# Where the next batch's projections stand among attention's score tiles

## The chip, the cores and the metric

The kernel runs on one core of one Trainium2 chip. The metric is the time of one execution on the device, in microseconds. Three runs of the kernel before took 1319.05, 1314.22 and 1311.92 us; the median is 1314.22 us.

## The reference, cut to what matters

Three blocks follow each other, all in float32, for 8 batches of 576 tokens.

```python
# 1: linear attention, per head (8 heads of 64, 128 features)
proj = x @ w_phi; proj -= max|proj|; phi = [exp(proj), exp(-proj)]
x1 = (phi(q) @ (phi(k).T @ v)) / (phi(q) @ sum(phi(k)) + 1e-6)
# 2: mixture of 4 attention experts, two of them taken per token
q, k, v = x1 @ wq[e], x1 @ wk[e], x1 @ wv[e]
a = softmax(causal(q @ k.T / 8)); ye = a @ v @ wo[e]
x2 = sum over the two best e of gate[e] * ye          # gate from x1 @ w_gate
# 3: token-shift feed-forward
xk, xr = mu * x2 + (1 - mu) * x2_shifted_by_one_token
out = sigmoid(xr @ w_r) * (relu(xk @ w_k) ** 2 @ w_v)
```

## The kernel before

Every product of block 2 and 3 is made of three passes over operands split into a high and a low part (`mm3`, L113). Four generators, called streams here, emit the work, and `weave` (L54) interleaves them by costs that each step returns:

- `favors` (L640) is block 1, for one batch after the other. Its tiles on TensorE (PE) are `pj` (projection by `w_phi`), `kv`, `tq` (transposes), `num` and `xt`; the last writes the batch's x1, split, into the store `XT`.
- `moe1` (L398) is block 2. Per batch and pair of experts (`ep` is 0 or 1) `qk_tasks` makes four tasks of 12 matmuls each into tiles `qk`, two for the queries, two for the keys; `v_tasks` makes five tasks of 12 matmuls into tiles `vp` (values and gate logits of all four experts), and `gate` turns the logits into weights on VectorE (DVE). Then `s_task` follows for each of 2 experts x 5 score tiles: scores `sc` on PE (L508, L509), mask and maximum on DVE (L518, L522), exponential on ScalarE (ACT, L528), reciprocal on DVE (L534), scaling on GpSimd (POOL, L540), transposes `at` back on PE (L547), and their copies into the tiles `at1h`/`ath` on ACT and `at1l`/`atl` on DVE. `av_task` multiplies the result by the values (`yp`, L582), and at a pair's end writes it to DRAM (`yd<-yt`, L603, on the SyncE queue, SP).
- `gates_keys` (L676) is the first product of block 3 (and `wo`, folded into its weights by `compose`, tiles `fo`). It goes by six chunks of 768 tokens. A chunk has 36 steps of 6 matmuls, tiles `rk`; before them `load_y` (L666) reads the chunk from DRAM into the one buffer `yc_` by four transfers issued on ACT's queue (L673). The buffer's name has a number per chunk: `yc__7491`, `yc__9926`, `yc__12263`, `yc__13856`, `yc__14845` and `yc__15948` are chunks 0 to 5 of the kernel before; the changed kernel has its own numbers. Each `rk` step's weights `wt` come by a transfer on ACT's queue too, its result goes to DRAM by SP (`kd<-z`).
- `moe2` (L727) is the rest: loads `kx<-kd` and `zs<-kd` on SP, relu and square on ACT, the split on DVE, and matmuls `vacc`, 192 a chunk. Its accumulators and most of its buffers take the place of block 2's, so it can't start before the last tile of `moe1` is done.

Within `moe1` the list of tasks sets the order (L611 to L638), and `skewed` (L41) overlaps the stages of neighbours in that list. What `weave` emits is a priority. The framework's own scheduler then sets each engine's order from priorities, dependencies and a model of durations, so moving a task in the list also moves other streams' instructions. `compose`, the weight decoding and `rk` carry a lower priority and fill PE where the others have nothing ready. Score tiles share two PSUM buffers; `qk`, `vp`, `at` and `yp` share two others until `favors` has ended, and after that `qk`, `vp` and `yp` have two of their own (`TAGS`, `LATE`, L31).

In the kernel before, the list has in front of the ten score tiles of a pair all projections of the following pair: four `qk` tasks in front of the first pair's score tiles, and four `qk`, five `vp` and the gate of the next batch in front of the second pair's.

Of the kernel before, what the change touches and what calls it, by code (L numbers as in the profile page):

```python
# [14 lines left out]
B, S, H, D = (8, 576, 8, 64)  # L15
# [61 lines left out]
def fused_kernel(ctx: ExitStack, tc: tile.TileContext, qT, kT, vx, wphi, wq, wk, wvg, wo, mu, w64, ident, cmask, tri, out):  # L77
# [25 lines left out]
    def evac(e, o, i):  # L103
        if e == 'a':
            nc.scalar.activation(o, i, AF.Copy)
        else:
            nc.vector.tensor_copy(o, i)
    state = {}

    def tg(n):  # L110
        return dict(tag=LATE.get(n, TAGS[n]) if 'favored' in state else TAGS[n], bufs=2)

    def mm3(ps, pairs, first=True, last=True):  # L113
        n = 3 * len(pairs)
        i = 0
        for sh, sl, mh, ml in pairs:
            for a, m in ((sh, mh), (sh, ml), (sl, mh)):
                nc.tensor.matmul(ps, a, m, start=first and i == 0, stop=last and i == n - 1)  # L118
                i += 1
# [278 lines left out]
    def moe1():  # L398

        def qk_tasks(b, ep):  # L400

            def one(isk, c):
                cs = slice(288 * c, 288 * c + 288)
                d = {}

                def mm():
                    if not isk and c == 0:
                        QS[b, ep] = pA.tile([P, 2, S], F32R, name='qs', tag='qs', bufs=2)
                        K1[b, ep] = pA.tile([P, 2, S], F32R, name='k1', tag='k1', bufs=2)
                        K2[b, ep] = K2Z[ep]  # L410
                    ps = psA.tile([P, 288], F32, name='qk', **tg('qk'))
                    wh, wl = (wkh, wkl) if isk else (wqh, wql)
                    mm3(ps, [(wh[:, ep, kt], wl[:, ep, kt], xh[kt, b][:, cs], xl[kt, b][:, cs]) for kt in (3, 2, 1, 0)])
                    d['ps'] = ps
                    if isk and c == 1 and (ep == 1):
                        read.add(b)
                    return 12 * 123

                def ev():
                    ps = d['ps']  # L420
                    for j in range(2):
                        r = slice(64 * j, 64 * j + 64)
                        o = slice(64 - 64 * j, P - 64 * j)
                        if isk:
                            k1 = K1[b, ep]
                            nc.scalar.activation(k1[r, j, cs], ps[r], AF.Copy)
                            nc.scalar.activation(k1[o, j, cs], ps[r], AF.Copy)
                            nc.vector.tensor_sub(K2[b, ep][r, j, cs], ps[r], k1[r, j, cs].bitcast(F32))
                        else:
                            q_ = QS[b, ep]  # L430
                            nc.scalar.activation(q_[r, j, cs], ps[r], AF.Copy, scale=0.125)
                            nc.vector.scalar_tensor_tensor(q_[o, j, cs], ps[r], 0.125, q_[r, j, cs].bitcast(F32), op0=OP.mult, op1=OP.subtract)
                return [(lambda: written.get(b, 0) == NHP * S, mm), ev]
            return [one(k, c) for k in range(2) for c in range(2)]

        def v_tasks(b):

            def one(t):
                m = P if t < 4 else 64
                d = {}  # L440

                def mm():
                    if t == 0:
                        VS[b] = VSP[b % 2]
                        LG[b] = pA.tile([P, 5, E], F32, name='lg', tag='lg', bufs=2)
                        nc.vector.memset(LG[b][64:P, 4, :], 0.0)
                    ps = psA.tile([P, 260], F32, name='vp', **tg('vp'))
                    cs = slice(P * t, P * t + m)
                    mm3(ps[:m], [(xh[kt, b][:, cs], xl[kt, b][:, cs], wvh[:, kt], wvl[:, kt]) for kt in (3, 2, 1, 0)])
                    d['ps'] = ps  # L450
                    return 12 * 109

                def ev():
                    ps = d['ps']
                    v4 = ps[:m, :256].rearrange('p (e d) -> p e d', e=E)
                    evac('a', VS[b][:m, t, :, 0:64], v4)
                    nc.vector.tensor_sub(VS[b][:m, t, :, 64:128], v4, VS[b][:m, t, :, 0:64].bitcast(F32))
                    nc.vector.tensor_copy(LG[b][:m, t, :], ps[:m, 256:260])
                return [mm, ev]
            return [one(t) for t in range(5)]  # L460

        def gate(b):

            def go():
                l = LG[b]
                sh4 = [P, 5, E, E]
                lf = l.unsqueeze(2).to_broadcast(sh4)
                le = l.unsqueeze(3).to_broadcast(sh4)
                g1 = pA.tile([P, 5, E, E], F32, name='g1', tag='g1')
                g2 = pA.tile([P, 5, E, E], F32, name='g2', tag='g2')  # L470
                nc.vector.tensor_tensor(g1, lf, le, op=OP.is_gt)
                nc.vector.tensor_tensor(g2, lf, le, op=OP.is_equal)
                nc.vector.tensor_mul(g2, g2, trs.rearrange('p (e f) -> p e f', e=E).unsqueeze(1).to_broadcast(sh4))
                nc.vector.tensor_add(g1, g1, g2)
                rk = pA.tile([P, 5, E], F32, name='rk', tag='rk')
                nc.vector.tensor_reduce(rk, g1, axis=AX.X, op=OP.add)
                mx = pA.tile([P, 5], F32, name='mx', tag='mx')
                nc.vector.tensor_reduce(mx, l, axis=AX.X, op=OP.max)
                sh3 = [P, 5, E]
                w_ = pA.tile([P, 5, E], F32, name='gw', tag='gw', bufs=2)  # L480
                nc.vector.tensor_sub(w_, l, mx.unsqueeze(2).to_broadcast(sh3))
                nc.scalar.activation(w_, w_, AF.Exp)
                nc.vector.scalar_tensor_tensor(w_, rk, 1.5, w_, op0=OP.is_lt, op1=OP.mult)
                sm = pA.tile([P, 5], F32, name='gs', tag='gs')
                nc.vector.tensor_reduce(sm, w_, axis=AX.X, op=OP.add)
                nc.vector.tensor_scalar_add(sm, sm, 1e-09)
                nc.vector.reciprocal(sm, sm)
                nc.vector.tensor_mul(w_, w_, sm.unsqueeze(2).to_broadcast(sh3))
                WT[b] = w_
            return [None, None, go]  # L490
# [116 lines left out]
        plan = []  # L607
# [3 lines left out]
        tasks = []  # L611
        due = []

        def flush(force=False):
            due.sort(key=lambda x: x[0])
            while due and (force or due[0][0] <= len(tasks)):
                tasks.append(due.pop(0)[1])
        tasks += qk_tasks(0, 0) + v_tasks(0) + [gate(0)]
        for n, (b, ep) in enumerate(plan):
            if n + 1 < len(plan):  # L620
                nb, nep = plan[n + 1]
                tasks += qk_tasks(nb, nep)
                if nep == 0:
                    tasks += v_tasks(nb) + [gate(nb)]
            for e in (2 * ep, 2 * ep + 1):
                for i in range(5):
                    tasks.append(s_task(b, e, i))
                    flush()
                    if i == 1:
                        due.append((len(tasks) + 5, av_task(b, e, 0)))  # L630
                    if i == 4:
                        due.append((len(tasks) + 4, av_task(b, e, 1)))
        while due:
            if due[0][0] > len(tasks):
                tasks.append([lambda: 2400])
            flush()
# [90 lines left out]
    def moe2():  # L727
# [62 lines left out]
        return skewed(tasks)  # L790
    clear_pads()
    fs, ms, rk, m2 = (favors(), skewed(moe1()), skewed(gates_keys()), moe2())
    for _ in range(3):
        next(fs)
# [57 lines left out]
```

## Time and profile before

| | |
|---|---|
| median of three runs | 1314.22 us |
| profiled execution | 1317.01 us, its span 1315.2 us |
| PE busy | 1257.2 us (96%) |
| VectorE / ScalarE / GpSimd busy | 881.4 / 732.5 / 411.6 us |
| matmuls | 9152 |

The span is the stretch from the first instruction to the last. Busy is the union of an engine's instructions; matmuls overlap, and so a stretch in which PE is busy throughout may still be paced by something else. `favors` starts its last `xt` at 822.1 us, the last `yp` of block 2 ends at 1051 us, and from then on only `rk` and `vacc` run on PE.

### The profile page before, as it was taken

Reading aid. Unit: us, or ns where it says so; the run is one execution under the profiler, and the core shown is the slowest. Engines: PE = TensorE matmul, PEld = TensorE weight load, DVE = VectorE, ACT = ScalarE, POOL = GpSimd, SP = SyncE. Lnnn points to the kernel's source line nnn. Section 1 sums busy time; section 2 is a strip of 40 time slices with the busy share of each in tenths; the row PEclk is TensorE's granted clock in tenths of the full one; section 3 lists DMA queues with packets and bytes.
Section 4 is the critical chain, followed back from the end, with each engine's and each line's share of the span. In section 5 each row is a group of like instructions: output and inputs, shape, how many; then the busy total and the mean of one; then the engine's idle time right before and its main releaser. Section 6 shows DMA issues by size and latency. Waiting matters only on the chain.

```text
span 1315.2 us, 26615 instructions
## 1 busy us (share of the span) xinstructions
PE 1257.2 (96%) x9152; PEld 1207.0 (92%) x9152; DVE 881.4 (67%) x2477; ACT 732.5 (56%) x1836; POOL 411.6 (31%) x570
## 2 busy tenths in 40 slices
PE   7999999999999999999999999898997989999998
PEld 7999899899999999899989999887996989999998
DVE  7776885887886777787777678565676745443442
ACT  5665675677676556565556556654454556343330
POOL 5541562655453335333433323322112200000000
PEclk9999999899999999999999999998997999999999
DMA  6322141324053435434554456578466897778741
GB/s 183 88 86 81 59 131 51 109 68 136 27 176 118 140 95 173 140 111 124 170 181 117 136 149 211 172 217 259 146 214 213 262 314 244 255 258 283 241 143 66
DMA packets 174358, 208.77 MB, mean 159 GB/s; under 512 B 19728, under 2 KB 159376, under 8 KB 174224
## 3 DMA queue, kind: packets, MB, share of 16 engines
q1 hardware_dynamic: 96656, 136.28, 31.7%
q10 hardware_dynamic: 77568, 70.79, 18.5%
q8 instruction: 74, 1.21, 0.4%
q14 instruction: 60, 0.49, 0.1%
HBM read 143.58 MB, written 63.44 MB: 157 GB/s over the span
## 4 chain that ended last, share of the span: by engine, by line
PE 76%; DVE 7%; DMA 5%; ACT 4%; POOL 3%; issue 2%; ACTq 1%; POOLq 0%; SPq 0%; DVEq 0%
PE vacc L118 14%; PE rk L118 14%; PE kv L328 9%; PE num L366 8%; PE qk L118 7%; PE vp L118 4%; PE at L547 3%; PE yp L582 3%; PE pj L276 3%; PE fo L118 2%; DMA kd<-z 2%; PE pj L278 2%; PE pj L277 2%; PE sc L508 2%; PE tq L350 2%
## 5 line engine op out<-in xcount | busy, mean ns | idle before, releaser
L118 PE MATMUL vacc<-XT,wvh 128*128 128x384 f32 x768 | 197.1, 338 | 2.1 <-DVE o L779 2.1
L101 POOL TENSOR_TENSOR lo<-raw,hi 128x256 fp32r<-128x256 f32 (+1 forms) x160 | 109.9, 691 | 259.9 <-ACT hi L98 217.5
L540 POOL TENSOR_SCALAR a<-a,rc,gw 128x128 f32<-128x128 f32 (+4 forms) x160 | 107.0, 671 | 202.6 <-DVE rc L534 109.8
L366 PE MATMUL num<-kvs,ph 128*128 128x65 f32 (+1 forms) x1280 | 142.8, 264 | 4.6 <-DVE xs L373 4.4
L366 PEld LDWEIGHTS num<-kvs,ph 128*128 128x128 f32 (+1 forms) x1280 | 137.5, 182 | 10.3 <-DVE xs L373 6.2
L118 PEld LDWEIGHTS vacc<-XT,wvh 128*128 128x128 f32 x768 | 139.8, 189 | 2.4 <-DVE o L779 2.4
L706 DVE TENSOR_TENSOR z<-rk,z 128x384 f32<-128x384 f32 x144 | 79.5, 552 | 74.3 <-PE rk L118 34.4
L286 DVE TENSOR_REDUCE m<-pj 128x4 f32<-128x512 f32 (+1 forms) x160 | 100.6, 631 | 41.9 <-PE pj L278 40.1
L118 PE MATMUL vacc<-XT,wvl 128*128 128x384 f32 x384 | 128.2, 338 | 0.0
L528 ACT ACTIVATE a<-sc,nm 128x128 f32<-128x128 f32 (+2 forms) x192 | 98.1, 514 | 45.4 <-DVE nm L522 16.1
L288 DVE TENSOR_TENSOR pm<-pj,m 128x512 f32<-128x512 f32 (+1 forms) x160 | 99.5, 627 | 1.4
L276 PE MATMUL pj<-wph,hi 128*128 128x256 f32 x288 | 92.4, 321 | 6.9 <-DVE wpl L101 3.8
L522 DVE TENSOR_REDUCE nm<-sc 128x1 f32<-128x128 f32 (+2 forms) x192 | 87.4, 468 | 3.9 <-PE sc L509 2.1
L98 ACT ACTIVATE hi<-raw 128x256 fp32r<-128x256 f32 (+1 forms) x160 | 61.8, 392 | 41.9 <-PE pj L277 19.3
L278 PE MATMUL pj<-wph,lo 128*128 128x256 f32 x288 | 84.0, 292 | 0.7 <-POOL lo L101 0.7
L277 PE MATMUL pj<-wpl,hi 128*128 128x256 f32 x288 | 83.5, 290 | 0.0
L547 PE MATMUL at<-idn,a 128*128 128x128 f32 (+2 forms) x480 | 74.5, 265 | 5.5 <-POOL a L540 2.9
L508 PE MATMUL sc<-k,qs 128*128 128x128 f32 (+2 forms) x192 | 66.2, 351 | 12.7 <-ACT a L528 12.6
L754 ACT ACTIVATE kx<-kx 128x768 f32<-128x768 f32 x48 | 40.2, 842 | 62.1 <-DMA kx<-kd 50.7
L563 ACT ACTIVATE at1h<-at 128x384 fp32r<-128x384 f32 (+3 forms) x128 | 53.5, 419 | 38.0 <-PE at L547 17.1
L118 PEld LDWEIGHTS vacc<-XT,wvl 128*128 128x128 f32 x384 | 72.5, 189 | 0.0
L100 DVE CAST XT<-kx 128x768 fp32r<-128x768 f32 x48 | 26.7, 557 | 65.4 <-PE vacc L118 53.6
(464 smaller groups left out, 3441.4 us busy)
## 6 DMA issues: line engine op xcount, KB each, us to landing
wt<-wf ACTq DMA_DIRECT2D x216, 256.0 KB, 3.7
kd<-z SPq DMA_DIRECT2D x144, 192.0 KB, 3.4
kx<-kd SPq DMA_DIRECT2D x48, 384.0 KB, 4.4
yd<-yt SPq DMA_DIRECT2D x16, 864.0 KB, 4.7
zs<-kd SPq DMA_DIRECT2D x24, 384.0 KB, 5.6
out_dram<-o SPq DMA_DIRECT2D x24, 384.0 KB, 4.6
raw<-in_kT_dram SPq DMA_DIRECT2D x64, 128.0 KB, 2.1
raw<-in_qT_dram SPq DMA_DIRECT2D x64, 128.0 KB, 2.2
```

The source lines that it names most:

```text
L101: (el or nc.vector).tensor_sub(lo, src, hi.bitcast(F32))
L118: nc.tensor.matmul(ps, a, m, start=first and i == 0, stop=last and i == n - 1)
L276: nc.tensor.matmul(o, hi[:, c], wph, start=True, stop=False)
L277: nc.tensor.matmul(o, hi[:, c], wpl, start=False, stop=False)
L278: nc.tensor.matmul(o, lo[:, c], wph, start=False, stop=True)
L286: nc.vector.tensor_reduce(m[:, :g], ps, axis=AX.X, op=OP.max, apply_absolute_value=True)
L288: nc.vector.tensor_sub(pm[:, :g * P].rearrange('p (g f) -> p g f', f=P), ps, m[:, :g].unsqueeze(2).to_broadcast([P, g, P]))
L328: nc.tensor.matmul(bank[:, r, :], d['kp'][:, r % 2, c0:c0 + P], d['v'][:, i + (lo_ > 0), r // 2, :], start=new and r == 0, stop=end, skip_ ...
L366: nc.tensor.matmul(ps[lo_:hi_, i, j, :], d['qp'][:, hf, c0 + lo_:c0 + hi_], kvs[hp, b][:, r * 65:(r + 1) * 65], start=hf == 0, stop=hf == 1)
L528: nc.scalar.activation(a[:m, k0:k1_], o, AF.Exp, bias=nm[:m, 0:1], scale=1.0, accum_out=sm[:m, n:n + 1])
L540: eng(asc).tensor_scalar(a[:m, :nk], a[:m, :nk], rc[:m], WT[b][:m, i, e:e + 1], op0=OP.mult, op1=OP.mult)
L547: nc.tensor.transpose(ps[:kw, jj * m:jj * m + m], d['a'][:m, jj * P:jj * P + kw], idn[:m, :m])
```

## The change

The list of `moe1`'s tasks is written in another order. The four `qk` tasks of a batch's second pair are put one by one behind the first four score tiles of the first pair. The next batch's `qk` tasks of its first pair, its five `vp` tasks and the gate are put behind the last score tile of the second pair, with the `av` tasks that fall due among them. No instruction on data is added or taken away.

```diff
--- before.py
+++ after.py
@@ -616,20 +616,22 @@
             while due and (force or due[0][0] <= len(tasks)):
                 tasks.append(due.pop(0)[1])
         tasks += qk_tasks(0, 0) + v_tasks(0) + [gate(0)]
-        for n, (b, ep) in enumerate(plan):
-            if n + 1 < len(plan):
-                nb, nep = plan[n + 1]
-                tasks += qk_tasks(nb, nep)
-                if nep == 0:
-                    tasks += v_tasks(nb) + [gate(nb)]
+        for b, ep in plan:
+            ahead = qk_tasks(b, 1) if ep == 0 else []
             for e in (2 * ep, 2 * ep + 1):
                 for i in range(5):
                     tasks.append(s_task(b, e, i))
                     flush()
+                    if ahead:
+                        tasks.append(ahead.pop(0))
                     if i == 1:
                         due.append((len(tasks) + 5, av_task(b, e, 0)))
                     if i == 4:
                         due.append((len(tasks) + 4, av_task(b, e, 1)))
+            if ep == 1 and b + 1 < B:
+                for t in qk_tasks(b + 1, 0) + v_tasks(b + 1) + [gate(b + 1)]:
+                    tasks.append(t)
+                    flush()
         while due:
             if due[0][0] > len(tasks):
                 tasks.append([lambda: 2400])
```

The first place is ACT at the load of chunk 4 (`yc__14845` before, `yc__14723` in the changed kernel; `a,sm<-sc,nm` is a score tile's exponential). Before:

```order
L673 DMA yc__14845<-yd_112 128x6x192
L563 ACTIVATE at1h<-at 128x3x128
L673 DMA yc__14845<-yd_112 128x6x192
L528 ACTIVATE a,sm<-sc,nm 64x512
L528 ACTIVATE a,sm<-sc,nm 64x64
L563 ACTIVATE at1h<-at 128x4x128
L721 DMA wt<-wf_116 128x2x256
L673 DMA yc__14845<-yd_113 128x6x192 x2
L528 ACTIVATE a,sm<-sc,nm 128x128
L528 ACTIVATE a,sm<-sc,nm 128x256
L563 ACTIVATE at1h<-at 128x4x64
L105 ACTIVATE yc<-yp 64x256
```

Now:

```order
L563 ACTIVATE at1h<-at 64x64
L723 DMA wt<-wf_116 128x2x256
L675 DMA yc__14723<-yd_112 128x6x192 x2
L105 ACTIVATE yc<-yp 64x320
L675 DMA yc__14723<-yd_113 128x6x192 x2
L98 ACTIVATE yt<-yf_172 128x288
L723 DMA wt<-wf_116 128x2x256
L98 ACTIVATE yt<-dl 128x576
L105 ACTIVATE z<-rk 128x384
L723 DMA wt<-wf_116 128x2x256
L723 DMA wt<-wf_117 128x2x256 x2
```

The load stood among the exponentials of score tiles; now it stands behind the last score tile of all, around the copy `yc<-yp` of the last product.

The second place is PE between chunks 2 and 3 (`yc__12263` and `yc__13856` before, `yc__12344` and `yc__13852` now). Before:

```order
L118 MATMUL rk<-yc__12263,wt 128x384 x6
L547 MATMUL at<-idn,a 128x64 x4
L547 MATMUL at<-idn,a 64x64
L118 MATMUL rk<-yc__12263,wt 128x384 x12
L508 MATMUL sc<-k_12013,qs 128x384
L509 MATMUL sc<-k2z_165,qs 128x384
...
L547 MATMUL at<-idn,a 128x128 x2
L508 MATMUL sc<-k_12013,qs 64x512
L509 MATMUL sc<-k2z_165,qs 64x512
L547 MATMUL at<-idn,a 128x128 x3
...
L118 MATMUL rk<-yc__13856,wt 128x384 x2
```

Now:

```order
L118 MATMUL rk<-yc__12344,wt 128x384 x6
L118 MATMUL vp<-wvh,XT 128x260
L118 MATMUL vp<-wvl,XT 128x260
...
L118 MATMUL vp<-wvl,XT 64x260
L118 MATMUL vp<-wvh,XT 64x260 x2
L118 MATMUL vp<-wvl,XT 64x260
L118 MATMUL vp<-wvh,XT 64x260
L118 MATMUL qk<-XT,wqh 128x288 x2
L118 MATMUL qk<-XT,wql 128x288
...
L547 MATMUL at<-idn,a 128x128 x2
L118 MATMUL rk<-yc__13852,wt 128x384 x2
```

Before, 36 matmuls `qk` and 12 `sc`, 10 `yp`, 10 `at` stand between the two chunks; now 48 `qk`, 24 `vp` and 3 `at`, and no score tile.

The third place is PE between chunks 3 and 4 (`yc__13856` and `yc__14845` before, `yc__13852` and `yc__14723` now). Before:

```order
L118 MATMUL rk<-yc__13856,wt 128x384 x12
L547 MATMUL at<-idn,a 128x128 x3
L508 MATMUL sc<-k_13825,qs 64x64
L509 MATMUL sc<-k2z_165,qs 64x64
L582 MATMUL yp<-ath,vsp_168 128x256
L582 MATMUL yp<-ath,vsp_168 128x128
...
L508 MATMUL sc<-k_13825,qs 64x512
L509 MATMUL sc<-k2z_165,qs 64x512
...
L509 MATMUL sc<-k2z_165,qs 64x64
L118 MATMUL rk<-yc__14845,wt 128x384 x2
L547 MATMUL at<-idn,a 128x128 x4
```

Now:

```order
L118 MATMUL rk<-yc__13852,wt 128x384 x12
L582 MATMUL yp<-at1h,vsp_168 128x320 x3
L582 MATMUL yp<-at1h,vsp_168 128x192
L118 MATMUL rk<-yc__13852,wt 128x384 x6
L582 MATMUL yp<-at1h,vsp_168 128x64
L582 MATMUL yp<-at1l,vsp_168 64x320 x3
L582 MATMUL yp<-at1l,vsp_168 64x192
L582 MATMUL yp<-at1l,vsp_168 64x64
L118 MATMUL vacc<-XT,wvh_13239 128x384 x2
...
L118 MATMUL vacc<-XT,wvh_13239 128x384 x2
L118 MATMUL vacc<-XT,wvl_13240 128x384
L118 MATMUL rk<-yc__14723,wt 128x384 x36
L118 MATMUL vacc<-XT,wvh_13239 128x384 x5
```

Before, 14 `sc`, 18 `at` and 18 `yp` stand between the chunks. Now 6 `yp` and 48 `vacc` do, and block 2 ends before chunk 4 begins: 432 matmuls `rk` stand behind the last `yp`, 300 before.

## Rows read from the trace of the kernel before

**Rows 1.** The page's first lines: span, and busy time of TensorE.

```profile
span 1315.2 us, 26615 instructions
...
PE 1257.2 (96%) x9152; PEld 1207.0 (92%) x9152; DVE 881.4 (67%) x2477; ACT 732.5 (56%) x1836; POOL 411.6 (31%) x570
```

**Rows 2.** Stretches: length, PE busy (matmuls), granted clock, DMA share, GB/s.

```profile
60.00:428.00 368.00, 355.78 (x2970) 0.98 0.30 94
428.00:840.00 412.00, 404.78 (x3191) 1.00 0.49 147
840.00:906.00 66.00, 59.67 (x377) 1.00 0.71 224
906.00:924.60 18.60, 12.87 (x72) 0.82 0.60 185
924.60:995.40 70.80, 68.41 (x446) 1.00 0.65 197
995.40:1012.00 16.60, 10.85 (x55) 0.69 0.76 265
1012.00:1053.00 41.00, 40.12 (x243) 0.96 0.74 227
1053.00:1090.00 37.00, 33.64 (x184) 0.95 0.93 319
1137.50:1155.80 18.30, 18.30 (x108) 1.00 1.06 362
```

**Rows 3.** Waits of PE, 840 to 1053 us: total, times, longest.

```profile
PE sc L508 <- ACT a L528: 10.0, 7, 3.2
PE rk L118 <- DVE z L706: 2.8, 4, 1.1
```

**Rows 4.** PE in order of time (start, us, what), inside 906 to 916 us.

```profile
910.30 0.41 PE L547 MATMUL at<-idn,a 128*128 128x128 f32 x2
913.95 0.69 PE L508 MATMUL sc<-k,qs 128*64 128x512 f32 x1 [3.23 <-ACT a L528]
```

**Rows 5.** ACT in order of time, the same stretch; ACTq is its queue.

```profile
907.60 1.73 ACTq L673 DMA_DIRECT2D yc__13856<-yd  x2
...
909.40 3.73 ACTq L673 DMA_DIRECT2D yc__13856<-yd  x1
913.23 0.58 ACT L528 ACTIVATE a<-sc,nm 128x384 f32<-128x384 f32 x1 [3.58 <-issue]
```

**Rows 6.** PE's last and first `rk` around four changes of chunk.

```profile
649.79 0.68 PE L118 MATMUL rk<-yc__7491,wt 128*128 128x384 f32 x3
660.22 0.42 PE L118 MATMUL rk<-yc__9926,wt 128*128 128x384 f32 x1
...
904.03 2.38 PE L118 MATMUL rk<-yc__12263,wt 128*128 128x384 f32 x12
924.53 0.51 PE L118 MATMUL rk<-yc__13856,wt 128*128 128x384 f32 x2
...
993.43 2.33 PE L118 MATMUL rk<-yc__13856,wt 128*128 128x384 f32 x12
1010.91 0.59 PE L118 MATMUL rk<-yc__14845,wt 128*128 128x384 f32 x2
...
1135.79 2.10 PE L118 MATMUL rk<-yc__14845,wt 128*128 128x384 f32 x11
1153.68 0.51 PE L118 MATMUL rk<-yc__15948,wt 128*128 128x384 f32 x2
```

**Rows 7.** The chain that ended last: start, us, what; three unbroken runs of matmuls.

```profile
877.13 1.58 PE qk L118 x12
...
933.03 2.87 PE vp L118 x24
...
1119.12 16.66 PE vacc L118 x96
```

**Rows 8.** DMA issues: count, KB each, median us to landing.

```profile
yc__14845<-yd ACTq DMA_DIRECT2D x4, 576.0 KB, 7.7
```

## The prediction

> **What bounds the kernel now.** I read the page's busy times first: PE is busy for 1257.2 of 1315.2 us [rows 1], no other engine for more than 67%. All matmuls stay, so the change can only move what PE loses. The table of stretches says where that is. Loss in a stretch is here its length less PE's busy time, plus its length times what the granted clock lacks to 1.00. The second part is a bound, since a slow clock costs nothing while PE idles anyway. By that, 60 to 428 us loses 12.2 + 7.4 us, 428 to 840 us 7.2, 840 to 1090 us 36.4 [rows 2]. So a fifth of the span holds more than half of what these rows lose: the part in which only score tiles, projections and `rk` are left for PE.
>
> Inside it, two short stretches stand out. From 906.0 to 924.6 us PE idles 5.7 us at a granted clock of 0.82, a loss of up to 9.1; from 995.4 to 1012.0 us it idles 5.8 us at 0.69, up to 10.9 [rows 2]. (A granted clock of 0.69 means that 62% of the stretch ran at 1.2 and not at 2.4 GHz, behind PE's idle time.) The list of `rk` matmuls tells what these stretches are: in both one chunk ends and the next has to be loaded into the single buffer, 18.1 and 15.2 us from the end of one to the start of the next [rows 6], and during that time PE's filler is gone. The waits name the partner: scores wait 10.0 us, 7 times, for an exponential to free their bank [rows 3]. One such wait lasts 3.23 us [rows 4], and ACT shows why the exponential is late: its queue spends 1.73 us on two and 3.73 us on another of the four load transfers, and the next exponential starts at 913.23 when they are through [rows 5].
>
> **The change part by part.** Nothing is removed or added. What moves are, per batch, 8 `qk` tasks (12 matmuls, two or four ACT copies and two DVE subtractions each), 5 `vp` tasks (12 matmuls, one ACT copy, two DVE operations) and a gate. They issue no transfer. But transfers move against them: the `yd` store on SP of a batch's second pair, which in the list stood behind the next batch's nine tasks, now stands in front of them, so a chunk's data is there earlier. The scheduler also puts other work between chunks now, and by the order of the built programs I go through the changes of chunk.
>
> Prices of cover come from unbroken runs: a `qk` matmul 1.58/12 = 0.132 us, `vp` 2.87/24 = 0.120, `vacc` 16.66/96 = 0.174 [rows 7]. What a chunk's change needs from the end of the last `rk` to the start of the next was 9.8, 18.1, 15.2 and 15.8 us [rows 6]; these are upper bounds, as the first `rk` may have been queued behind other work, and the smallest is the nearest to a bound from below.
>
> 1. Chunk 3 to 4 leaves the score tiles. Between them stood 50 short matmuls of score tiles, with their exponentials behind the load; now it happens when block 2 is over. The 10.9 us fall to what an equal length costs in the stretch behind it, (0.9 + 1.6) us x 16.6/41 = 1.0 [rows 2]. Term: -9.9. Bounds 0 and -10.9.
>
> 2. Chunk 2 to 3 now has 48 `qk` and 24 `vp`, 6.3 + 2.9 = 9.2 us, and no score tile. Against a need of 15.2 us, the row with the nearest DMA load, 6.0 us of waiting are left of 9.1. Term: -3.1. Bounds: need 9.8, only 0.6 left, -8.5; need 18.1, 8.9 left, -0.2. ACT still holds the four transfers, and now copies of `vp` and `qk` queue behind them; PE has two banks of 12 matmuls, 2.9 us, before it feels that.
>
> 3. The change from 3 to 4 moves to the hand-over to `vacc`. There 48 `vacc`, 8.3 us, and 6 `yp`, some 0.6 us, stand between; need 15.2, so 6.3 us are waited. Bounds: 0.9 (need 9.8) and 9.2 (need 18.1). The hand-over's own loss, 3.4 + 1.9 us in 1053 to 1090 us [rows 2], stays. Term: +6.3. Queued behind the first waiting `rk` on PE are 36 `rk` and then all `vacc`; on ACT two of the load's transfers stand before the copy `yc`, two before the split `yt` from which the last store and then the `kx` loads follow.
>
> 4. Chunk 4 to 5 had 92 `vacc` between, 16.0 us, and PE did not idle [rows 2]: the need of 15.8 was just hidden. Now 66 `vacc` stand there, 11.5 us. If that cover is gone, 4.3 us are waited. Term: +4.3. Bounds 0 (need 9.8) and 6.6 (need 18.1).
>
> 5. Chunks 0 to 1 and 1 to 2 have 54 and 54 matmuls between them for 57 and 62, 11 fewer of about 0.13 us. Term: +1.5; bounds 0 and +4 for a need above the cover already, which the first one's 9.8 us suggest.
>
> 6. The rest of 840 to 1053 us loses 6.3 + 2.4 + 2.5 = 11.2 us [rows 2]. Behind the last `xt` the order has 98 score matmuls for 120, so a fifth less of the chains that make these waits. Term: -2.0; bounds +4 (468 matmuls `rk` as filler there for 563) and -6.
>
> 7. Before 840 us 26.8 us are lost [rows 2]. Spread projections put more work between tiles that share two PSUM buffers: pairs of `qk`, `vp`, `at`, `yp` tiles with under 1.5 us of PE work between one use of a buffer and the next fall from 24 to 15 in the order, counted at such prices. No row prices that; a tenth is my choice. Term: -2.0; bounds +8 and -8.
>
> Sum: -9.9 - 3.1 + 6.3 + 4.3 + 1.5 - 2.0 - 2.0 = -4.9 us. The profiled execution took 1317.0 us, 2.8 above the median of the three runs; 1317.0 - 4.9 = 1312.1, and against the median 1314.2 - 4.9 = 1309.3. I forecast **1309 us**. About 0.5%, 6.6 us, is what a measurement of this kernel can tell from no change, so the forecast is a small gain at the edge of that.
>
> **The rivals.** *A larger gain.* The load's need is nearer to 9.8 us, as from chunk 0 to 1, because no exponentials and fewer `wt` transfers share ACT's queue with it. For it speaks that the two long changes are those in which score tiles held PE and so the next `rk`; against it that 15.8 us were needed among `vacc` as well. Terms 2 to 5 become -8.5, +0.9, 0 and +1.5, the sum -20.0, the time 1294; with half of it 1300.
>
> *No change.* The waits are the same ones in other places: terms 2 and 6 at nothing, 3 and 4 at 9.2 and 6.6 from a need of 18.1. Then -9.9 + 9.2 + 6.6 + 1.5 - 2.0 = +5.4, or with term 4 as forecast +3.1: 1317 to 1320.
>
> *Slower: the hand-over.* Chunk 4's load is 4 x 576 KB, 2.36 MB [rows 8]. It now falls where the `kx` and `zs` loads of chunk 0 start, a stretch that moves 319 GB/s at a DMA share of 0.93 already [rows 2]. There 2.36 MB more take 7.4 us, and `kx` lands by that much later while the load itself needs 18.1. PE would wait 9.2 + 7.4 us, and at the clock of the 906 us stretch lose 3.3 more: 19.9 in place of 6.3, a sum of +8.7 and 1323 us. It decides as soon as `kx` lands after the 36 `rk`, some 15 us behind the load's issue. Against it: chunk 5's load at a share of 1.06 cost PE nothing [rows 2]. The Trainium skill ("DMA: Bandwidth & Descriptors", section "Issuing engines are not separate DMA queues") says that transfers started by several engines run on the same 16 DMA engines and interleave, which speaks for this rival. The same section calls the time to initiate a transfer "usually small relative to the DMA itself"; here 3.73 us for one issue stand beside a median landing of 7.7 us, and the measurement decides.
>
> **How the numbers follow.** Forecast, 1303 to 1314 us: 0.46. Larger gain, 1292 to 1303: 0.22. No change, 1314 to 1320: 0.17. Slower: 0.15. Faster by over 0.5% is the larger gain and four tenths of the forecast's case, 0.41; slower by over 0.5% is the hand-over and a little of the third case, 0.17; the rest, 0.42, is within 0.5%. The range of 1297 to 1321 us leaves out the far end of each side; the forecast's own is 1303 to 1314.
>
> **What would show it.** Right: the `sc` waits for an exponential behind 840 us fall from 10.0 to under 4 us; PE idles some 6 us between the 48 `vacc` and the first `rk` of chunk 4, and some 4 us behind the 66 `vacc` before chunk 5; the last `yp` ends some 35 us before its 1051 us, 23 us of that being the 132 `rk` that move behind it. The forecast is wrong if the hand-over loses over 15 us, if chunk 5's first `rk` isn't waited for, or if the loss before 840 us moves by more than 8 us.

## The result and the profile after

The changed kernel takes 1302.86 us (median of 6 runs, 1298.90 to 1306.01) against 1313.42 us: a ratio of 0.9913 over all runs (the two medians alone give 0.9920), 95% interval 0.9885 to 0.9940. Six more runs of it gave 1299.41 us and 0.9893 (0.9868 to 0.9918). So it is faster by about 1%; the forecast was 1309 us, the range 1297 to 1321.

The page of the changed kernel shows as many matmuls as before and a span 18.1 us shorter. Some of that is these two executions: the profiled one was the fastest of its six runs, the one of before 3.6 us above its median.

```profile
span 1297.1 us, 26595 instructions
...
PE 1249.1 (96%) x9152; PEld 1204.4 (93%) x9152; DVE 884.2 (68%) x2477; ACT 733.2 (57%) x1836; POOL 412.5 (32%) x570
```

The table of stretches of the changed kernel (columns as in [rows 2]; 811.2 us is its last `xt`, 1008.5 its last `yp`):

```profile
60.00:428.00 368.00, 359.96 (x3059) 1.00 0.32 100
220.00:260.00 40.00, 38.38 (x325) 1.00 0.26 83
428.00:811.20 383.20, 378.12 (x3020) 1.00 0.45 134
811.20:1008.50 197.30, 178.45 (x1148) 0.98 0.69 212
837.20:850.20 13.00, 9.46 (x55) 0.87 0.77 248
931.80:946.00 14.20, 9.96 (x77) 1.00 0.65 206
1007.00:1020.00 13.00, 11.27 (x59) 0.87 1.00 337
1134.60:1146.20 11.60, 11.60 (x68) 1.00 1.03 334
```

The same view of the kernel before, two stretches that its table in [rows 2] does not have (822.2 us is its last `xt`, 1051 its last `yp`):

```profile
220.00:260.00 40.00, 35.14 (x260) 0.91 0.28 97
822.20:1051.00 228.80, 206.81 (x1295) 0.96 0.68 212
```

Read with the prediction's measure (length less busy, plus length times what the clock lacks), 60 to 428 us lost 12.2 + 7.4 us [rows 2] and now loses 8.0 at a full clock. The stretch with no `favors` left lost 22.0 + 9.2 us and now loses 18.9 + 3.9. So the trace shows two gains, 11.6 and 8.4 us, and the larger is the one that I had all but left out.

Where the early one is, the groups of instructions in 220 to 260 us show (name, count, busy and mean, then idle time before and who ended it). Before:

```profile
L366 PE MATMUL num<-kvs,ph 128*128 128x65 f32 (+1 forms) x95 | 12.0, 287 | 2.5 <-DVE xs L373 2.5
...
L118 PE MATMUL fo<-wth,sw 128*128 128x256 f32 x28 | 6.8, 316 | 1.1 <-ACT wth L98 1.1
```

After:

```profile
L366 PE MATMUL num<-kvs,ph 128*128 128x65 f32 (+1 forms) x96 | 10.8, 262 | 0.0
L118 PE MATMUL vp<-wvh,XT 128*128 128x260 f32 (+1 forms) x40 | 8.1, 292 | 0.4 <-DVE k2z L428 0.4
```

Before, the last of the next batch's `vp` matmuls starts at 218.4 us and the next `qk` at 265.7, so for 46 us PE ran no projection: block 1's chain (`num` waits for `xs`, which DVE makes of the last `num`) had only `fo` and score tiles between its links, PE got through 260 matmuls and its clock fell (0.91 granted). Now 120 matmuls `qk` and `vp` stand there, `num` waits for nothing, and PE gets through 325. By the same measure this stretch loses 8.5 us before and 1.6 now, 6.8 of the 11.6.

The three changes of chunk that the prediction spoke of, by the changed kernel's first and last `rk` (start, length):

```profile
930.68 1.21 PE L118 MATMUL rk<-yc__12344,wt 128*128 128x384 f32 x6
945.99 0.59 PE L118 MATMUL rk<-yc__13852,wt 128*128 128x384 f32 x2
...
1005.88 1.24 PE L118 MATMUL rk<-yc__13852,wt 128*128 128x384 f32 x6
1019.46 1.75 PE L118 MATMUL rk<-yc__14723,wt 128*128 128x384 f32 x9
...
1134.35 0.34 PE L118 MATMUL rk<-yc__14723,wt 128*128 128x384 f32 x1
1146.03 0.62 PE L118 MATMUL rk<-yc__15948,wt 128*128 128x384 f32 x2
```

Beside [rows 6], the gaps from the end of one to the start of the next are 14.1, 12.3 and 11.3 us, for 18.1, 15.2 and 15.8. Behind the 66 `vacc` PE did not idle at all (11.60 of 11.60 us busy).

### The profile page after: what moved, and what is told of

It is laid out like the page before. It is cut to its first block, busy times and chain, and to the rows that moved or that the text cites. A ratio compares the mean times of both kernels' runs of the same rounds, so it can differ in the third digit from the quotient of the medians.

```text
span 1297.1 us, 26595 instructions
## 1 busy us (share of the span) xinstructions
PE 1249.1 (96%) x9152; PEld 1204.4 (93%) x9152; DVE 884.2 (68%) x2477; ACT 733.2 (57%) x1836; POOL 412.5 (32%) x570
## 4 chain that ended last, share of the span: by engine, by line
PE 83%; DVE 6%; DMA 4%; ACT 2%; POOL 2%; issue 1%; ACTq 1%; SPq 0%; DVEq 0%; POOLq 0%
PE rk L118 16%; PE vacc L118 16%; PE kv L328 10%; PE num L366 8%; PE qk L118 6%; PE vp L118 4%; PE yp L582 3%; PE at L547 3%; PE pj L276 3%; PE fo L118 3%; PE pj L278 2%; PE pj L277 2%; PE tq L350 2%; PE sc L508 2%; PE sc L509 2%
## 5 line engine op out<-in xcount | busy, mean ns | idle before, releaser
L118 PE MATMUL vacc<-XT,wvh 128*128 128x384 f32 x768 | 201.2, 338 | 3.8 <-DVE XT L100 2.0
L105 ACT ACTIVATE z<-rk 128x384 f32<-128x384 f32 x72 | 35.2, 489 | 63.0 <-PE rk L118 53.2
```

## The experiments

Two theories stood against each other. *Loads*: the gain comes from the tail, since a chunk's load no longer meets score tiles. *Early*: it comes from the part before 822 us, where projections between score tiles fill PE. Each list of tasks is built anew by the scheduler, so each run also tells how much of an effect survives another order.

**Half of the change.** One kernel deals out the second pair's `qk` tasks and leaves the next batch's tasks in front of the second pair's score tiles; the other does the reverse. The first (written here in its effect; the lines under the last `if` go with it):

```diff
             ahead = qk_tasks(b, 1) if ep == 0 else []
+            if ep == 1 and b + 1 < B:
+                tasks.extend(qk_tasks(b + 1, 0) + v_tasks(b + 1) + [gate(b + 1)])
...
-            if ep == 1 and b + 1 < B:
```

The other, where those of the next batch stay behind the last score tile:

```diff
             ahead = qk_tasks(b, 1) if ep == 0 else []
+            if ep == 0:
+                tasks.extend(ahead)
+                ahead = []
```

> Half of the change: the four qk tasks of a batch's second pair are dealt out among the first pair's score tiles; the next batch's nine tasks and the gate stay in front of the second pair's score tiles, as before. In the order, chunk 3 to 4 changes at the hand-over to vacc (9.0 us of other work between), but chunk 2 to 3 still changes among score tiles (10 sc, 8 at, 10 yp and 24 qk, 6.8 us). Theory 'loads' (the gain comes from chunk loads that no longer meet score tiles): the hand-over part is there, some -9 us, chunk 2 to 3 costs 9 us as before, so 1304 to 1308 us, ratio 0.993 to 0.996. Theory 'early' (the gain comes from the part before 822 us, where projections between score tiles fill PE and keep its granted clock up): about half of the whole change's gain, ratio 0.995 to 0.997, with the loss in 60 to 428 us falling from 19.6 us to some 13.

Measured: 1345.71 us, ratio 1.0239 (1.0198 to 1.0281). Slower, and neither theory had that. Most of it is lost before the last `xt`: 60 to 428 us loses 16.7 + 18.4 us, and 428 us to the last `xt` at 859 us 8.5 + 12.9, where the kernel before loses 6.3.

> The other half: the next batch's nine tasks and the gate go behind the second pair's last score tile; the second pair's four qk tasks stay together in front of the first pair's score tiles. In the order, chunk 3 to 4 changes among the last score tiles (14 at, 10 yp, 4 sc, 3.1 us of work between). Theory 'loads': the wait stays there, so the tail gains little, 1309 to 1314 us, ratio 0.997 to 1.000, and PE loses 8 us or more around that load. Theory 'early': ratio 0.995 to 0.997, with the loss in 60 to 428 us near 13 us.

Measured: 1311.31 us, ratio 1.0018 (0.9992 to 1.0045): no difference. Both halves lose more before 428 us than the kernel before. The stretches of the first, and with them one in which its clock stayed down:

```profile
60.00:428.00 368.00, 351.32 (x2836) 0.95 0.27 85
...
392.00:409.50 17.50, 16.55 (x73) 0.51 0.15 46
```

and of the second:

```profile
60.00:428.00 368.00, 353.49 (x2875) 0.95 0.30 95
220.00:260.00 40.00, 39.85 (x338) 1.00 0.30 99
```

The halves do not add up to the whole; the part before 428 us gains only with both. The stretch of 220 to 260 us, though, is filled by the second half alone (338 matmuls); that kernel loses its time in other places, as from 280 to 297.5 us, where its granted clock is 0.51. Why it does is not shown.

**The change in half of the batches.** Both places of the change, for batches 0 to 3 (shown) or for batches 4 to 7 (`b >= 4`), the others as before.

```diff
-            ahead = qk_tasks(b, 1) if ep == 0 else []
+            ahead = []
+            if ep == 0:
+                ahead = qk_tasks(b, 1)
+                if not (b < 4):
+                    tasks.extend(ahead)
+                    ahead = []
+            elif b + 1 < B and not (b < 4):
+                tasks.extend(qk_tasks(b + 1, 0) + v_tasks(b + 1) + [gate(b + 1)])
...
-            if ep == 1 and b + 1 < B:
+            if ep == 1 and b + 1 < B and (b < 4):
```

> Both halves of the change, for batches 0 to 3 alone; batches 4 to 7 stand as before. In the order chunk 3 to 4 changes among the last score tiles (14 at, 14 yp, 4 sc, 3.6 us of work between), chunk 2 to 3 among score tiles too (7.3 us). Theory 'early': nearly the whole gain, ratio 0.990 to 0.994, and the loss in 60 to 428 us at 8 to 10 us as in the changed kernel. Theory 'loads': nearly nothing, 1309 to 1314 us, ratio 0.997 to 1.000.

Measured: 1317.89 us, ratio 1.0044 (1.0028 to 1.0060).

> Both halves of the change, for batches 4 to 7 alone; batches 0 to 3 stand as before. In the order chunk 3 to 4 changes among the last score tiles (10 at, 14 yp, 6 sc, 3.7 us of work between) and chunk 2 to 3 with 24 qk, 9 at, 14 yp, 4 sc between (6.0 us). Theory 'early': nothing, ratio 0.998 to 1.002, and the loss in 60 to 428 us near 19 us as before. Theory 'loads': a part, since score tiles and projections still alternate but the loads meet score tiles: ratio 0.995 to 0.999, with PE losing 6 us or more around chunk 4's load. A ratio near 0.991 would say that neither is the cause, and that it is the alternation in the last batches alone.

Measured: 1324.76 us, ratio 1.0107 (1.0083 to 1.0131).

By time both theories fall. The traces save half of *early*. At least the first 3900 matmuls of `e3_early` stand in the same order as the changed kernel's, and as many of `e4_late` in that of the kernel before, so they repeat the early part (3900 matmuls take 490 to 500 us). `e3_early`, 220 to 260 us and its stretch without `favors`:

```profile
220.00:260.00 40.00, 38.40 (x324) 1.00 0.25 81
817.00:1024.40 207.40, 181.11 (x1114) 0.94 0.69 217
```

`e4_late`:

```profile
220.00:260.00 40.00, 35.13 (x274) 0.96 0.28 99
827.00:1033.00 206.00, 183.32 (x1156) 0.95 0.68 214
```

The early gain is the list's, not chance: 38.4 us busy again with the new list, 35.1 with the old. But `e3_early` gives it back in the tail, which loses 26.3 + 12.4 us, and `e4_late`, with the new list there, loses 22.7 + 10.3, no less than the old list's 22.0 + 9.2. In both, three changes of chunk fall behind the last `xt` and in front of the last `yp` (at 833, 932 and 1011, and at 830, 934 and 1016 us); the kernel before has two, the changed one two and the third at the hand-over.

**Who issues the load.** The four transfers of a chunk's load go to SP's queue.

```diff
-load_y(c, d['y'], nc.scalar)
+load_y(c, d['y'], nc.sync)
```

> The kernel before, with the four transfers that load a chunk issued on SP's queue in place of ACT's. Theory 'ACT held up' (a change of chunk among score tiles costs because the issues stand in front of exponentials on ACT): the score matmuls' wait for an exponential behind 840 us falls from 10.0 us to under 3, each change of chunk among score tiles loses under 4 us, ratio 0.988 to 0.994. Theory 'filler gone' (it costs because no rk matmul can stand between score tiles until the chunk is there, whoever issues the load): the changes lose 6 us or more as before, ratio 0.997 to 1.002.

Measured: 1307.51 us, ratio 0.9962 (0.9938 to 0.9985), between the two. The waits of PE from 820 to 1050 us in this kernel:

```profile
PE rk L118 <- DVE z L706: 5.2, 7, 2.5
PE sc L508 <- ACT a L528: 4.7, 6, 1.9
```

The scores' wait for exponentials halves, from 10.0 us [rows 3] to 4.7. The two changes of chunk behind the last `xt`, 2 to 3 and 3 to 4, are these stretches:

```profile
913.05:924.78 11.73, 10.86 (x85) 1.00 0.87 281
993.61:1002.69 9.08, 5.69 (x35) 0.84 0.99 321
```

They lose 0.9 and 4.8 us where the kernel before lost 9.1 and 10.9, so in this trace most of that price is gone with the issues on ACT. That is no clean proof: the order is another one too (from chunk 2 to 3 stand 48 `vp` and 24 `qk`, and 6 `sc` for 12), and what 'filler gone' is worth was not measured by itself. The whole gains less than these stretches, in part because the 39 us behind the last `yp` lose 6.6 + 3.5 us for 3.4 + 1.6.

> The changed kernel, with the chunk's load issued on SP's queue. In the order chunk 3 to 4 changes with 94 vacc between, 1 to 2 and 2 to 3 among projections and few score tiles. Theory 'ACT held up': another 3 to 6 us gained, ratio 0.986 to 0.989. Theory 'filler gone': as the changed kernel, ratio 0.989 to 0.994.

Measured: 1287.95 us, ratio 0.9829 (0.9799 to 0.9859): 12 to 15 us off the two medians of the changed kernel (1299.41 and 1302.86; by the ratios 8 to 11), for 6 (by the ratio 5) off the kernel before, and more than either theory said. This version beats both. What ACT's issues cost in the changed kernel its own trace shows, between chunks 2 and 3 on ACT:

```profile
931.92 1.57 ACTq L675 DMA_DIRECT2D yc__13852<-yd  x3
933.54 0.38 ACT L105 ACTIVATE vsp<-vp 128x256 fp32r<-128x256 f32 x1 [2.73 <-PE vp L118]
933.57 2.48 ACTq L675 DMA_DIRECT2D yc__13852<-yd  x1
936.14 2.42 ACTq L723 DMA_DIRECT2D wt<-wf  x1
938.61 0.38 ACT L105 ACTIVATE vsp<-vp 64x256 fp32r<-64x256 f32 x1 [4.68 <-issue]
```

and on PE, the next thing in its queue:

```profile
939.65 0.50 PE L118 MATMUL qk<-XT,wqh 128*128 128x288 f32 x2 [3.23 <-DVE lg L458]
```

For 4.68 us ACT issued transfers while two projection tiles waited to be copied, and PE waited 3.23 us for the bank (the row names `lg` because DVE's reads of the tile, which follow ACT's copy, come last). The new list has no exponential behind the load, but copies of projections instead. With the load on SP the same change of chunk has as many `vp`, `qk` and `at` between and loses 0.7 us in place of 4.2:

```profile
925.80:936.16 10.36, 9.63 (x75) 1.00 0.89 283
```

**No loads.** Chunks 1 to 5 are not loaded; every chunk multiplies chunk 0's data, so the other chunks' own part of block 3's first product is left out in these two kernels. Buffer, wait and transfers of the load are gone.

```diff
-d['y'] = pR.tile([P, 2, 2, 3, HC], F32R, name='yc_', tag='y')
-load_y(c, d['y'], nc.scalar)
+if c == 0:
+    kept['y'] = pR.tile([P, 2, 2, 3, HC], F32R, name='yc_', tag='y')
+    load_y(c, kept['y'], nc.scalar)
+d['y'] = kept['y']
```

> The kernel before without the loads of chunks 1 to 5 (every chunk multiplies chunk 0's data): no wait for the buffer, no transfer, and rk matmuls at hand at all times. Theory 'loads': the losses at the changes of chunk (9.5 and 9.7 us behind 822 us, 2.7 us before) go, 1290 to 1300 us, ratio 0.982 to 0.990. Rival 'score chains' (the tail loses because softmax chains are long, and the changes of chunk only happen to lie there): 1304 to 1313 us, ratio 0.993 to 1.000.

Measured: 1299.81 us, ratio 0.9911 (0.9879 to 0.9943).

> The changed kernel without the loads of chunks 1 to 5, in the same way. If the gain of the whole change is the sum of a part before 822 us (some 10 us, which two pairs of profiles show) and fewer losses at changes of chunk (some 8 us in the profiles), then without loads the two lists should differ by the first part alone: this kernel 8 to 11 us faster than the kernel before without loads, 1282 to 1291 us, ratio 0.976 to 0.983 to the kernel before. If the tail's gain comes from alternation as such, the two differ by more than 14 us. If the part before 822 us is chance, they differ by less than 4 us.

Measured: 1283.48 us, ratio 0.9785 (0.9754 to 0.9815), 16.3 us under its partner. The two traces, 60 to 428 us and the stretch between the last `xt` and the last `yp`; old list:

```profile
60.00:428.00 368.00, 354.81 (x2990) 0.99 0.30 95
220.00:260.00 40.00, 35.16 (x275) 0.96 0.29 99
821.00:1051.40 230.40, 218.67 (x1411) 0.99 0.72 224
```

New list:

```profile
60.00:428.00 368.00, 360.28 (x3063) 1.00 0.32 100
220.00:260.00 40.00, 38.39 (x324) 1.00 0.25 81
808.00:1002.40 194.40, 184.65 (x1206) 0.99 0.68 208
```

This rules out *loads* as the whole cause. They do cost: without them the old list's tail loses 11.7 + 2.3 us in place of 22.0 + 9.2. But the new list is ahead by at least as much without them as with them, so its lead can't be only that its loads lie better. The early part gives 9.2 us here (13.2 + 3.7 against 7.7). Of the tail *loads* is half right: there the new list is 8.4 us ahead with the loads and 2.3 without, so most of the tail's gain does go with them. By its time this pair falls into the branch of the expectation that blames alternation in the tail (over 14 us), and the rows do not bear that out: besides 9.2 and 2.3, the part from 428 us to the last `xt` gives 2.8 us and the 39 us behind the last `yp` 3.1. No run took these two apart.

**Parts again, with the load on SP.** The early and the late half of the batches, each with the edit above.

> The change for batches 0 to 3 alone, and a chunk's load issued on SP's queue. The kernel before with that load on SP took 1307.5 us, the changed one 1288.0. If the two halves of the change add up and only the place of ACT's issues spoilt the early half's result (+0.4% with the load on ACT), this takes off the part before 822 us, some 9 to 12 us: 1295 to 1300 us, ratio 0.986 to 0.990. If the halves don't add up for another reason (the list of the late batches sets where the changes of chunk fall, 3 to 4 among the last score tiles with 4.2 us of work between), 1302 to 1309 us, ratio 0.992 to 0.997, with the loss of 60 to 428 us near 21 us all the same.

Measured: 1297.19 us, ratio 0.9899 (0.9872 to 0.9925). With ACT free of the load, the early half alone brings the ratio from 0.9962 to 0.9899, 8 us. Its trace, before 428 us and from the last `xt` to the last `yp`:

```profile
60.00:428.00 368.00, 359.61 (x3057) 1.00 0.32 100
808.00:1011.40 203.40, 182.09 (x1132) 0.94 0.72 225
```

Against the old list with the load on SP (`sp_before`), the part before 428 us loses 5.1 us less and the part from there to the last `xt` 8 less; the tail loses 14 more, and the 39 us behind the last `yp` 9 less. So the early gain shows in the time, but that it comes out near the forecast is partly luck of the later stretches. (The 21 and 30 us that these two expectations and the last one name for 60 to 428 us are no reading of that stretch, which loses 8.0 us in the changed kernel and 13.5 in `sp_before`; they are near what is lost from the start to the last `xt`, 20 and 29 us.)

> The change for batches 4 to 7 alone, and a chunk's load issued on SP's queue. If the halves add up: the rest of the 19.5 us between 1307.5 and 1288.0, 8 to 11 us, so 1296 to 1300 us, ratio 0.987 to 0.991, with 60 to 428 us losing near 30 us as before. If they don't: 1304 to 1312 us, ratio 0.993 to 0.999, with 5 us or more lost at each change of chunk behind 822 us.

Measured: 1310.03 us, ratio 0.9990 (0.9968 to 1.0012): the late half alone gains nothing. Early and late together gain 1.3% over the old list (0.9829 against 0.9962), the parts 0.6% and nothing; the parts still don't add up, and why the late half helps only behind the early one stays open. The changes of chunk fall elsewhere in each order, and no run fixed them while the list changed.

**Two queues for the load**, in search of a faster version: the high part on SP's queue, the low part on ACT's.

```diff
-load_y(c, d['y'], nc.scalar)
+load_y(c, d['y'], (nc.sync, nc.scalar))
...
-    q.dma_start(y[:, h, :, :, o:o + n].bitcast(F32), yd[b][:, h, :, :, s0:s0 + n])
+    q[h].dma_start(y[:, h, :, :, o:o + n].bitcast(F32), yd[b][:, h, :, :, s0:s0 + n])
```

> The changed kernel with each chunk's load shared out: the high part on SP's queue, the low part on ACT's. Looked for as a faster version. If what counts is the time from the last rk of a chunk to the next (issue and landing), two queues shorten the issue and it takes 1284 to 1288 us, ratio 0.979 to 0.983. If what counts is that ACT issues none of it, it lies between the changed kernel (1302.9) and the one with SP alone (1288.0), ratio 0.984 to 0.990.

Measured: 1286.92 us, ratio 0.9821 (0.9791 to 0.9851): the same as with SP alone.

**The changed kernel once more.**

> The changed kernel once more, unchanged, for a second profile: the first profiled execution took 1298.9 us, the fastest of its six runs, and differs from the kernel before's by 18.1 us where the medians differ by 10.6. If the 7.5 us between are chance of two profiled executions, this one's profile shows 60 to 428 us losing near 21 us again (the list's own effect), and a longer slow-clock time elsewhere than the first's 10 us, with a median of 1300 to 1306 us. If the part before 428 us was the chance, it loses 25 us or more there.

Measured: 1299.41 us, ratio 0.9893 (0.9868 to 0.9918). Its second profile:

```profile
60.00:428.00 368.00, 360.24 (x3062) 1.00 0.32 100
220.00:260.00 40.00, 38.39 (x325) 1.00 0.25 83
810.00:1008.40 198.40, 180.77 (x1150) 0.97 0.69 210
```

The early part repeats to 0.3 us, so it was not chance; the tail loses 17.6 + 6.0 us for 18.9 + 3.9.

## Why the prediction was right, and which of its terms were not

The direction, the range and term 1's place were right; the size was less than half of the measured one, because errors of both signs stood in the sum. That the sum came out inside the range is in part luck: two waits that never came, 10.6 us in all, hid an early gain that the sum had at 2.0. By two of the signs that the prediction gave itself its working is wrong: chunk 5's first `rk` isn't waited for, and 60 to 840 us loses 17.2 us for 26.8, a move of 9.6. The rival of a larger gain, at 0.22, has the measured time at its edge and terms 3 and 4 about right, but its ground, a need near 9.8 us, gives -8.5 for term 2, which came to -4.9, and says nothing of the early part. Point by point, in the prediction's measure:

- **Term 1 (chunk 3 to 4 leaves the score tiles), -9.9: confirmed.** The stretch's 10.9 us are gone, and the scores' wait for an exponential, 10.0 us before, has no row any more in the list of PE's waits from 837 to 1008 us, which begins with 3.2 us of `qk` (line 118) for `lg`.
- **Term 2 (chunk 2 to 3), -3.1: right in sign, the mechanism wrong.** 4.2 us are lost there for 9.1, a term of -4.9. But PE did not wait for the chunk. It waited for a projection's bank, behind ACT's issues; the two banks that I counted as cover were too few.
- **Term 3 (chunk 3 to 4 at the hand-over), +6.3, and term 4 (chunk 4 to 5), +4.3: wrong, no wait came.** The failed step is the need. I took 15.2 and 15.8 us from [rows 6], having called them upper bounds in the same paragraph. PE had other work in front of the next `rk` in both, so these rows tell how long the queue was, not how long the load takes. In the changed kernel 12.3 and 11.3 us were enough. With the lower row, 9.8 us, the terms would have been +0.9 and 0. PE's 1.7 us of idle time at the hand-over were for the last tile of block 2, and the slower rival had nothing to stand on.
- **Term 5 (chunks 0 to 1 and 1 to 2), +1.5: too small.** From chunk 1 to 2 the changed kernel loses 3.5 + 1.7 us for 0.4 before: that change had the end of `favors` beside it at 812 us and now falls behind it, at 837. The count was wrong as well: by the traces 65 and 78 matmuls stood at these two changes and 70 and 54 stand there now, not 57 and 62, and 54 and 54.
- **Term 6 (the rest of the tail), -2.0: nothing of it shows.** 31.2 less 9.1 and 10.9 were 11.2 us; 22.8 less 5.2 and 4.2 are 13.4, so 2.2 more.
- **Term 7 (before 840 us), -2.0 with bounds of 8 either way: mis-sized, the largest error.** It is -11.6 us in 60 to 428 us alone, and 6 to 12 in every pair of profiles with the old and the new early list (the least, 5.6, with the load on SP). I had priced it by a count of short distances between tiles that share banks. The row that would have priced it was there to ask for: a stretch of 40 us with 260 matmuls and a clock of 0.91, in a part that does 144 to 177 matmuls in every other 20 us. The prediction has stretches of that fineness only behind 840 us.

The whole span in that measure, cut at 60 us, 428 us, the last `xt`, the last `yp` and some 39 us behind it:

| Stretch | loss before, us | loss now, us | difference |
|---|---|---|---|
| up to 60 us | 8.2 | 7.0 | -1.2 |
| 60 to 428 us (term 7) | 19.6 | 8.0 | -11.6 |
| 428 us to the last `xt` (terms 5 and 7) | 6.3 | 5.1 | -1.2 |
| last `xt` to last `yp` (terms 1, 2, 5, 6) | 31.2 | 22.8 | -8.4 |
| the hand-over (term 3) | 4.9 | 4.5 | -0.4 |
| the rest (term 4, whose change of chunk loses nothing now as before) | 5.9 | 8.5 | +2.6 |

The differences make some -20 us, beside 18.1 us between the two profiles; what the clock lacks counts in full in this measure, which makes it a bound. The table tells where the time went; the experiments show the early gain as the new list's own, and leave open how much of the rest another order would keep.

## What to carry to other kernels

Look at the whole span in stretches as fine as the pattern of the work, by matmuls a stretch, before deciding where a reordering acts: idle time of 4.9 us in 40 hides in a share of 96%. A gap between two uses of a buffer is what a load needs only where the engine idled until the load's end; otherwise take the shortest gap in the trace. And a transfer issued from an engine's queue is work of that engine: take it to a queue with nothing urgent behind it before weighing orders of tasks (here 0.6 to 0.8% from one word with the new list, 0.4% with the old).

## What the runs showed of the hardware

- An issue on ACT's queue took 0.37 us at best and up to 3.73 us [rows 5], and ACT's own work stood behind it. The four issues of one load took 2 to 3 us in all for chunks 0 to 2 and 4 to 6 us for chunks 3 to 5, in the kernel before and in the changed one.
- A clock that has fallen can stay down under load. In `e1_second_pair` PE waited 2.2 us for an exponential (`sc`) up to 392.95 us, and from 392 us on the granted clock was 0.51 for 17.5 us in which PE was busy 16.55, nearly all of it at 1.2 GHz; a run of narrow `kv` matmuls that took 268 ns each just behind this stretch stood in it at 412 (one row of PE in order of time, one of its groups of instructions):

```profile
392.95 0.69 PE L508 MATMUL sc<-k,qs 128*128 128x384 f32 x1 [2.22 <-ACT a L528]
...
L328 PE MATMUL kv<-vx__5827,ph 128*128 128x65 f32 x16 | 3.5, 412 | 0.0
```

That kernel, slower by 2.4%, had a granted clock of 0.95 from 60 to 428 us, where the kernel before had 0.98 [rows 2]. `e2_next_batch` had 0.95 there too and took no longer than the kernel before, so this stretch's clock alone does not make the 2.4%.
